# Four attention layers on one core: VectorE's exponentials in the final layer's first chunk taken spaced and in halves, with memory of their own from the second layer on

## The chip, the core and the metric

The kernel runs on one core of a Trainium2 chip. Its engines are TensorE (PE, with its weight loads listed apart as PEld), VectorE (DVE), ScalarE (ACT), GpSimd (POOL) and SyncE (SP), which work side by side, each on its own list of instructions in order. The metric is the device time of one execution in microseconds. Three runs of the kernel before took 2165.64, 2168.42 and 2171.80 us, median 2168.42.

## The reference

Four attention layers follow each other, each with a layer norm in front and a residual sum behind; x has 2048 positions of 640 values, there are 32 heads of 20. The first and third (A) see a window of 256 earlier positions, the second and fourth (B) see all positions.

```python
def _A_ref(x, wqkv, wo):                       # _B_ref is the same without the mask
    qkv = ((x @ wqkv).reshape(B, S, 3, H, Dh)).transpose(2, 0, 3, 1, 4)
    q, k, v = qkv[0], qkv[1], qkv[2]
    scores = jnp.einsum("bhqd,bhkd->bhqk", q, k) * (Dh ** -0.5)
    mask = (idx[:, None] - idx[None, :] >= 0) & (idx[:, None] - idx[None, :] < 256)
    p = _softmax(jnp.where(mask[None, None], scores, -1e9), axis=-1)
    o = jnp.einsum("bhqk,bhkd->bhqd", p, v)
    return o.transpose(0, 2, 1, 3).reshape(B, S, D) @ wo

x = x + _A_ref(_layernorm(x), A_wqkv, A_wo)
x = x + _B_ref(_layernorm(x), B_wqkv, B_wo)
x = x + _A_ref(_layernorm(x), A_wqkv, A_wo)
x = x + _B_ref(_layernorm(x), B_wqkv, B_wo)
```

## The kernel before

Layers are numbered 0 to 3 in the code; 1 and 3 see all keys. Positions are cut into four chunks c of 512, keys into 16 blocks of 128, heads into eight groups g of four. A unit is one (layer, chunk, group), for some units with only a part of the keys: layer 1's chunk 0 is done in four parts of four key blocks, layer 3's chunk 0 in two parts, key blocks 0 to 11 and 12 to 15, since the last chunk of the layer below is finished late. What such a part yields is kept in the tile `raw_o` (L864 to L875) until the last part adds to it.

All units stand in one list (L752 to L768), and a main loop (from L1371) goes through their score banks. A bank is 128 keys by 512 positions for one head. One step of the loop issues the scores of up to three banks on TensorE (L1416), one exponential over all of them on ScalarE (L1442), and, some steps later, the matmuls with the values (L1475). PSUM has eight banks: steps take banks 0 to 2 and 3 to 5 in turn, bank 7 collects the output, and bank 6 is, from the later parts of layer 1's chunk 0 on, the only one for all other work on TensorE.

That other work is a list of tasks, run by `pump`, `choose` and `advance` a little in each step, ordered by when they are needed: layer norm and its transposes (`t_ln`), projections of q, k (`t_block`, matmuls of `by_columns` at L315) and v (`t_v`), and the output projection (`t_out`, sum at L587). Each ends with an eviction from PSUM by VectorE (L339), and the next one can take bank 6 only after it. `rate` sets how much of it a step gets. Where TensorE would have too little to do, `unread` adds matmuls that nobody reads.

VectorE also computes exponentials itself, for a few pairs of banks that are taken from the end of a unit's list (`side_take`), so that ScalarE's step covers two banks instead of three. For one pair VectorE does two conversions to fixed point, one per bank (L989), and a chain of four operations over both banks, 1024 columns: `fraction` (L1005), `square` (L1013), `cubic` (L1017) and `whole` (L1023). The result is used as any other exponential (L1065). Memory of a chain: two tiles `xi` for the fixed-point numbers, one tile `t`, and a list of output tiles. `side_giver` says which unit gives the next pair, `side_work` decides by `state["lag"]`, an estimate of how far VectorE is behind, whether a chain's next operation is issued now.

Before the change there are two regimes. In layer 1 from its chunk 1 on (`side_early`), the chain's memory is all in `raw_o`, which layer 3's first unit needs again; `cubic` and `whole` are issued as two halves of 512 columns, at least GAP_1 = 5 steps lie between two banks taken, and the limits LAG_1, WORK_1 and PRE_1 are low. From layer 3's chunk 0, group 4, on (`side_start`), the memory is in three of the five tiles `xnT` for normalised chunks and in tiles that the windowed layers no longer need; operations are whole, there is no gap, and the limits LAG, WORK are higher. Between them, in layer 3's groups 0 to 3 and in the small units of layer 2 that stand there, VectorE takes no banks.

Of the kernel before, what the change touches and what calls it, by code (L numbers as in the profile page):

```python
# [18 lines left out]
P = 128  # L19
# [5 lines left out]
KD = D // P  # L25
# [20 lines left out]
KEEP = 30  # L46
HALF = True
HALF_3 = False
MOST_1 = 64
# [10 lines left out]
def kernel(  # L60
# [22 lines left out]
    xtp = pool("xtp", 5)  # L83
# [31 lines left out]
    kas = [ka_all[:, n, :] for n in range(KA)]  # L115
    qa_all = big.tile([P, QA, C], BF16, name="qa", tag="qa")
# [211 lines left out]

    def used(l, c):
        users[l, c] -= 1  # L330
        if users[l, c] == 0:
            live["xnT"] -= 1

# [76 lines left out]
    def t_ln(l, c):  # L410
# [19 lines left out]
        xt = xtp.tile([P, KD, C], BF16, name="xnT", tag="xnT")  # L430
# [432 lines left out]
    def finish_unit(u):  # L863
        l, c, g = u.l, u.c, u.g  # L864
        state["lag"] += 0.7
        if u.part and u.part[1] < NT:
            if not part_o:
# [12 lines left out]
        while len(tails) >= 3:  # L880
            require(tails[0].name)
        end = (l, c) == (3, NC - 1) and g >= G - 2
        before = g - 2 if end else g - 3
        if packed(l, c) and before >= 0:
            require(("tail", l, c, before))
        oT = ons[l, c][:, 5 + g % 3 if packed(l, c) and not end else g, :]
        if u.part:
            nc.vector.tensor_tensor(out=oT, in0=part_o["t"][:, g, :], in1=op, op=ALU.add)
        else:
            nc.vector.tensor_copy(out=oT, in_=op)  # L890
        ended_units.append((l, c, g, oT))
# [8 lines left out]
        "xi": deque(), "chain": deque(), "out": deque(), "late": False, "early": False,  # L900
        "half": None, "at": 0, "last": 0,
    }
    givers = [u for u in units if not u.windowed and (u.l, u.c) != (1, 0)]

    def side_tiles(xi, t, outs):

        side["xi"].extend(xi)
        side["t"] = t
        side["out"].extend(outs)

    def side_start():

        assert live["xnT"] <= 2 and not side["chain"] and side["half"] is None
        tl = [xtp.tile([P, KD, C], BF16, name="xnT", tag="xnT") for _ in range(3)]
        live["xnT"] += 3
        f = [v[:, 0:4, :].rearrange("p a b -> p (a b)").bitcast(F32) for v in tl]
        side["xi"].clear()
        side["out"].clear()
        outs = [ka_all[:, KA - 6 + 2 * n : KA - 4 + 2 * n, :] for n in range(3)]
        outs += [qa_all[:, 2 * n : 2 * n + 2, :] for n in range(2)]  # L920
        side_tiles(f[0:2], f[2].bitcast(F16)[:, 0 : 2 * C], outs)
        side["late"] = True

    def side_early():

        b = part_o["t"]
        f = [b[:, 2 * n : 2 * n + 2, :].rearrange("p a b -> p (a b)") for n in range(2)]
        outs = [b[:, n, :].bitcast(BF16).rearrange("p (a b) -> p a b", a=2) for n in range(5, G)]
        side_tiles(f, b[:, 4, :].bitcast(F16), outs)
        side["early"] = True  # L930

    def side_giver():

        if not side["late"] and state["tick"] < side["last"] + GAP_1:
# [3 lines left out]
        if not side["xi"]:  # L938
# [3 lines left out]
        for n in range(side["at"], min(side["at"] + 3, len(givers))):  # L942
# [3 lines left out]
            if not side["late" if u.l == 3 else "early"]:  # L946
                return None
            if u.l == 1 and len(u.aside) >= MOST_1:
                continue
            if len(u.rest) >= (KEEP if len(u.rest) + len(u.aside) < u.size else 12):  # L950
# [46 lines left out]
    def chain(u, xi):  # L997
# [23 lines left out]
        def whole(h):  # L1021
# [5 lines left out]
            if h.stop == 2 * C:  # L1027
                side["xi"].append(xi)
# [3 lines left out]
        halves = (slice(0, C), slice(C, 2 * C)) if HALF and (u.l == 1 or HALF_3) else every  # L1032
# [24 lines left out]
    def side_values(u, wait):  # L1057

        pairs = side_out.get(id(u), ())
        while u.valued < len(pairs) and pairs[u.valued][1] + wait <= state["tick"]:  # L1060
# [8 lines left out]
            side["out"].append(pt)  # L1069
# [166 lines left out]
    def first_ln():  # L1236
# [3 lines left out]
        xt = xtp.tile([P, KD, C], BF16, name="xnT", tag="xnT")  # L1240
# [55 lines left out]
    with tc.manual_schedule():  # L1296
# [74 lines left out]
        while ended is None or t < ended + 8:  # L1371
# [3 lines left out]
            if flow:  # L1375
                if not side["early"] and state["unit"] >= index[1, 1, 0, None]:
                    side_early()
                if (
                    not side["late"] and state["unit"] >= index[3, 0, 4, PARTS[3][0]]
                    and live["xnT"] <= 1 and not live["qa"] and not live["ka"]  # L1380
# [4 lines left out]
                giver = side_giver() if state["lag"] < (LAG if side["late"] else LAG_1) else None  # L1385
# [106 lines left out]
            if n_b and not side["late"]:  # L1492
# [82 lines left out]
```

## Time and profile before

| | |
|---|---|
| median of three runs | 2168.42 us |
| the profiled execution's time | 2167.19 us |
| its span, first to last instruction | 2165.5 us |
| TensorE clock granted, mean share | 0.998 |
| first layer and layer 1's chunk 0 | 0 to 492 us |
| layer 1 from chunk 1, with layer 2's units among it | 492 to 1268 us |
| layer 3, chunk 0, groups 0 to 3, keys 0 to 11 | 1268 to 1354 us |
| layer 2, chunk 3 (eight small units) | 1354 to 1397 us |
| layer 3, chunk 0, groups 4 to 7, keys 0 to 11 | 1397 to 1475 us |
| layer 3, chunk 0, the last four key blocks | 1475 to 1541 us |
| layer 3, chunks 1 to 3 | 1541 to 2155 us |

The stages are found by the exponentials: the steps of the loop, in order, are the exponentials on ScalarE in order of time. A row of the profile's windows has the window, its length, and the busy time of TensorE, of its weight loads, of VectorE, ScalarE and GpSimd. Busy time below the length of the window is time in which that engine stood. A row of waits has the waiting engine and line, who ended the wait, and how long it was in total, how often and at most.

### The profile page before, as it was taken

What the parts mean: (1) busy time and instruction counts of PE and PEld (TensorE: products, weight loads), DVE (VectorE), ACT (ScalarE), POOL (GpSimd) and SP (SyncE); (2) the same over time, 40 slices, a digit from 0 to 9 for tenths busy, and PEclk for the clock granted to TensorE, in tenths of its full rate; (3) what the DMA queues carried; (4) which work ended last, traced back from release to release, by engine and by line L of the source; (5) the groups of instructions that cost most, each with busy time, mean ns of one, the idle gap of its engine ahead of it and who ended that gap; (6) DMA issues with size and microseconds to landing.
All of it is one profiled execution on the core that took longest, in us unless ns stands there. A gap on an engine that the chain in (4) does not pass through costs nothing. (4 is left out here: it accounts for less than half of the span.)

```text
span 2165.5 us, 73279 instructions
## 1 busy us (share of the span) xinstructions
PE 1924.8 (89%) x31759; PEld 754.6 (35%) x31759; DVE 1488.7 (69%) x2625; ACT 2086.1 (96%) x1717; POOL 485.9 (22%) x953
## 2 busy tenths in 40 slices
PE   8999999988889898888988989888898898888898
PEld 4444443433333333333333433332332222222222
DVE  5656665426666776776767733676779887888896
ACT  7889899999999999999999999989999999999997
POOL 6665546110122113410053112511000000000000
PEclk9999999999999999999999999999999999999999
DMA  6223233322211323112241133112121111111100
GB/s 204 76 84 107 75 92 101 81 80 64 79 45 27 84 61 90 41 41 61 56 112 33 37 86 99 39 42 77 53 60 44 35 36 42 32 33 39 42 30 17
DMA packets 88418, 137.29 MB, mean 63 GB/s; under 512 B 20766, under 2 KB 63486, under 8 KB 88094
## 3 DMA queue, kind: packets, MB, share of 16 engines
q1 hardware_dynamic: 68878, 79.43, 13.9%
q0 software_dynamic: 19216, 53.17, 8.3%
q8 instruction: 249, 4.08, 0.8%
q14 instruction: 75, 0.61, 0.1%
HBM read 99.52 MB, written 27.79 MB: 59 GB/s over the span
## 5 line engine op out<-in xcount | busy, mean ns | idle before, releaser
L1442 ACT ACTIVATE pt<-ps 128x1536 bf16<-128x1536 f32 (+2 forms) x1641 | 2051.7, 1406 | 46.4 <-PE ps L1416 35.5
L1416 PE MATMUL ps<-qt,kt 32*128 32x512 bf16 x3914 | 544.6, 383 | 59.8 <-ACT pt L1442 52.5
L315 PE MATMUL ps<-masks,ident 128*32 128x512 bf16 x5652 | 505.6, 384 | 96.6 <-ACT pt L1442 47.5
L1475 PE MATMUL ps<-pt,vt 128*21 128x512 bf16 x3774 | 375.9, 386 | 1.8 <-issue 1.0
L1416 PEld LDWEIGHTS <-kt 32*128 32x128 bf16 x3914 | 154.7, 91 | 460.2 <-issue 440.4
L315 PEld LDWEIGHTS <-ident 128*32 128x32 bf16 x5652 | 180.3, 94 | 278.9 <-issue 253.5
L1515 POOL TENSOR_SCALAR_AFFINE_SELECT pt<-pt 128x256 bf16<-128x256 bf16 (+2 forms) x506 | 217.1, 451 | 187.6 <-ACT pt L1442 175.3
L315 PE MATMUL ps<-xnT,wqk 128*32 128x512 bf16 x3320 | 225.2, 381 | 11.9 <-DMA wqk<-in_B_wqkv_dram 2.1
L339 DVE CAST st<-ps 128x512 bf16<-128x512 f32 x134 | 92.5, 690 | 143.9 <-PE ps L315 143.6
L1475 PEld LDWEIGHTS <-vt 128*21 128x21 bf16 x3774 | 93.4, 89 | 260.1 <-issue 256.3
L989 DVE TENSOR_SCALAR xnT<-ps 128x512 int32<-128x512 f32 x210 | 144.1, 687 | 34.6 <-PE ps L971 27.5
L315 PE MATMUL ps<-wop,on 128*32 128x320 bf16 x3712 | 160.5, 300 | 5.7 <-DVE x_sb L587 3.9
L1526 DVE TENSOR_TENSOR pt<-pt,masks 128x256 bf16<-128x256 bf16 (+3 forms) x268 | 113.4, 438 | 46.5 <-ACT pt L1442 44.3
L315 PEld LDWEIGHTS <-on 128*32 128x32 bf16 x5760 | 122.3, 95 | 63.7 <-issue 29.8
L1416 PE MATMUL ps<-qa,ka 32*128 32x384 bf16 (+2 forms) x1408 | 118.0, 276 | 22.5 <-ACT pt L1442 19.1
L587 DVE TENSOR_TENSOR x_sb<-x_sb,ps 128x320 bf16<-128x320 bf16 x120 | 58.2, 485 | 101.6 <-PE ps L315 101.1
L1185 DVE TENSOR_TENSOR on<-on,ps 128x512 bf16<-128x512 bf16 x128 | 86.4, 684 | 59.2 <-PE ps L315 57.0
L315 PE MATMUL ps<-wv,xnT 128*32 128x320 bf16 x2560 | 116.0, 301 | 9.0 <-DVE vs L339 2.0
L315 PEld LDWEIGHTS <-wqk 128*32 128x32 bf16 x3320 | 83.2, 96 | 96.0 <-issue 38.1
L989 DVE TENSOR_SCALAR raw_o<-ps 128x512 int32<-128x512 f32 x112 | 76.8, 686 | 47.3 <-PE ps L1416 46.8
L890 DVE CAST on<-ps 128x512 bf16<-128x512 f32 x112 | 76.7, 685 | 37.9 <-PE ps L1475 30.7
L554 POOL DMA_DIRECT2D k_d<-st x75 | 42.5, 567 | 225.7 <-DVE st L339 213.0
(99 smaller groups left out, 1797.9 us busy)
## 6 DMA issues: line engine op xcount, KB each, us to landing
vt<-v_d SPq DMA_DIRECT2D x48, 336.0 KB
kt<-k_d SPq DMA_DIRECT2D x192, 80.0 KB
wqk<-in_B_wqkv_dram POOLq DMA_DIRECT2D x80, 160.0 KB, 3.5
wqk<-in_A_wqkv_dram POOLq DMA_DIRECT2D x70, 160.0 KB, 3.6
k_d<-st POOLq DMA_DIRECT2D x75, 128.0 KB, 2.5
q_d<-st POOLq DMA_DIRECT2D x75, 128.0 KB, 2.3
qt<-q_d SPq DMA_DIRECT2D x384, 20.0 KB
v_d<-vs POOLq DMA_DIRECT2D x16, 336.0 KB, 3.0
```

The source lines that it names most:

```text
L315: nc.tensor.matmul(out_[r], lhsT=lhsT[:, r], rhs=rhs, start=start, stop=stop)
L339: nc.vector.tensor_copy(out=out_, in_=in_)
L554: nc.gpsimd.dma_start(out=dst, in_=staging.pop())
L587: nc.vector.tensor_tensor(out=xv, in0=had, in1=yp, op=ALU.add)
L890: nc.vector.tensor_copy(out=oT, in_=op)
L989: nc.vector.tensor_scalar(out=xi.bitcast(I32)[:, i * C : (i + 1) * C], in0=z, scalar1=SCALE * LOG2E * FIX, scalar2=127.5 * FIX, op0=ALU.mu ...
L1185: nc.vector.tensor_tensor(out=oT, in0=oT, in1=zb, op=ALU.mult)
L1416: nc.tensor.matmul(sp[:, i, col * P : (col + qn) * P], lhsT=u.k(kc, j), rhs=u.q(j, q0, qn), start=True, stop=True,)
L1442: nc.scalar.activation(out=pt[:, i:k, b0 * P :], in_=sp[:, i:k, b0 * P :], func=ACT.Exp, scale=SCALE,)
L1475: nc.tensor.matmul(op[32 * j : 32 * j + VW, q0 * P : (q0 + qn) * P], lhsT=u.v(kc, j), rhs=pg[:, i, col * P : (col + qn) * P], start=(first ...
L1515: nc.gpsimd.affine_select(out=v, in_=v, compare_op=ALU.is_gt if later else ALU.is_ge, fill=0.0, base=0, pattern=[[0, k - i], [-1 if later ...
L1526: nc.vector.tensor_tensor(out=pt_[:, i:k, cols], in0=pt_[:, i:k, cols], in1=mv_, op=ALU.mult)
```

## The change

VectorE's exponentials get memory that doesn't depend on `raw_o` being free. The five tiles `xnT` become one tile `xt_all` with five slices that the kernel hands out itself (`take_xt`, `used`). Near the end of layer 1's chunk 0 `side_first` takes three of the slices for good: two `xi`, one `t` and two outputs. When chunk 0 of layer 1 is done, `side_lend` adds the eight slices of `raw_o` as outputs; at layer 3's first unit `side_retire` takes them back, those in use as soon as they come home (`side_home`). `side_start` only adds outputs in the tiles of the windowed layers.

The regime is now chosen by `freely()`, true from layer 3's chunk 1 on. Until then everything is as in layer 1: gap, low limits, halves. So layer 3's groups 0 to 3 and layer 2's last units among them get VectorE exponentials too, and groups 4 to 7 get them spaced and halved. Units of fewer than 32 banks (the last four key blocks) give none. A unit gives its first pair only while it has at least KEEP_1 = 39 banks left (KEEP = 30 from chunk 1 of layer 3 on, as before); the bound MOST_1 is gone. When a unit has fewer than 12 banks left, its chain's limit rises to WORK.

```diff
--- before.py
+++ after.py
@@ -44,9 +44,10 @@
 PRE = 1.3
 PRE_1 = 0.8
 KEEP = 30
+KEEP_1 = 39
 HALF = True
+BEFORE = 0
 HALF_3 = False
-MOST_1 = 64
 GAP_1 = 5
 QA = 4
 
...
@@ -113,6 +113,7 @@
     qts = [big.tile([P, C], BF16, name=f"qt{n}", tag=f"qt{n}") for n in range(4)]
     ka_all = big.tile([P, KA, C], BF16, name="ka", tag="ka")
     kas = [ka_all[:, n, :] for n in range(KA)]
+    xt_all = big.tile([P, 5, KD, C], BF16, name="xnT", tag="xnT")
     qa_all = big.tile([P, QA, C], BF16, name="qa", tag="qa")
     qas = [qa_all[:, n, :] for n in range(QA)]
 
@@ -326,10 +327,19 @@
 
     users = {}
 
+    xt_free = deque(range(5))
+    xt_n = {}
+
+    def take_xt(l, c):
+
+        xt_n[l, c] = xt_free.popleft()
+        return xt_all[:, xt_n[l, c]]
+
     def used(l, c):
         users[l, c] -= 1
         if users[l, c] == 0:
             live["xnT"] -= 1
+            xt_free.append(xt_n.pop((l, c)))
 
     def evac(out_, in_):
         if state["act"]:
...
@@ -886,6 +897,8 @@
         oT = ons[l, c][:, 5 + g % 3 if packed(l, c) and not end else g, :]
         if u.part:
             nc.vector.tensor_tensor(out=oT, in0=part_o["t"][:, g, :], in1=op, op=ALU.add)
+            if l == 1 and g == G - 1:
+                side_lend()
         else:
             nc.vector.tensor_copy(out=oT, in_=op)
         ended_units.append((l, c, g, oT))
@@ -897,45 +910,67 @@
 
     side_out = {}
     side = {
-        "xi": deque(), "chain": deque(), "out": deque(), "late": False, "early": False,
-        "half": None, "at": 0, "last": 0,
+        "xi": deque(), "chain": deque(), "out": deque(), "late": False, "on": False,
+        "half": None, "at": 0, "last": 0, "lent": None,
     }
-    givers = [u for u in units if not u.windowed and (u.l, u.c) != (1, 0)]
-
-    def side_tiles(xi, t, outs):
-
-        side["xi"].extend(xi)
-        side["t"] = t
+    givers = [u for u in units if not u.windowed]
+    away = []
+
+    def side_home(kind, v):
+
+        if any(v is a for a in away):
+            away[:] = [a for a in away if a is not v]
+        else:
+            side[kind].append(v)
+
+    def side_retire(parts):
+
+        for v in parts:
+            for kind in ("xi", "out"):
+                if any(v is a for a in side[kind]):
+                    side[kind] = deque(a for a in side[kind] if a is not v)
+                    break
+            else:
+                away.append(v)
+
+    def side_first():
+
+        for n in range(2, 5):
+            xt_free.remove(n)
+        live["xnT"] += 3
+        f = xt_all[:, 2:5].rearrange("p n a b -> p (n a b)")
+        f = [f[:, n * 2 * C : (n + 1) * 2 * C] for n in range(7)]
+        b = xt_all[:, 2:5].rearrange("p n a b -> p (n a b)")
+        outs = [f[n].rearrange("p (a b) -> p a b", a=2) for n in (5, 6)]
+        side["xi"].extend(b[:, 4 * n * C : 4 * (n + 1) * C].bitcast(F32) for n in range(2))
+        side["t"] = f[4].bitcast(F16)
         side["out"].extend(outs)
+        side["on"] = True
+
+    def side_lend():
+
+        b = part_o["t"]
+        side["lent"] = [b[:, n, :].bitcast(BF16).rearrange("p (a b) -> p a b", a=2) for n in range(G)]
+        side["out"].extend(side["lent"])
 
     def side_start():
 
-        assert live["xnT"] <= 2 and not side["chain"] and side["half"] is None
-        tl = [xtp.tile([P, KD, C], BF16, name="xnT", tag="xnT") for _ in range(3)]
-        live["xnT"] += 3
-        f = [v[:, 0:4, :].rearrange("p a b -> p (a b)").bitcast(F32) for v in tl]
-        side["xi"].clear()
-        side["out"].clear()
         outs = [ka_all[:, KA - 6 + 2 * n : KA - 4 + 2 * n, :] for n in range(3)]
         outs += [qa_all[:, 2 * n : 2 * n + 2, :] for n in range(2)]
-        side_tiles(f[0:2], f[2].bitcast(F16)[:, 0 : 2 * C], outs)
+        side["out"].extend(outs)
         side["late"] = True
 
-    def side_early():
-
-        b = part_o["t"]
-        f = [b[:, 2 * n : 2 * n + 2, :].rearrange("p a b -> p (a b)") for n in range(2)]
-        outs = [b[:, n, :].bitcast(BF16).rearrange("p (a b) -> p a b", a=2) for n in range(5, G)]
-        side_tiles(f, b[:, 4, :].bitcast(F16), outs)
-        side["early"] = True
+    def freely():
+
+        return state["unit"] >= index[3, 1, 0, None]
 
     def side_giver():
 
-        if not side["late"] and state["tick"] < side["last"] + GAP_1:
+        if not freely() and state["tick"] < side["last"] + GAP_1:
             return None
         if side["half"] is not None:
             return side["half"][0]
-        if not side["xi"]:
+        if not side["xi"] or not side["on"]:
             return None
         while side["at"] < len(givers) and not givers[side["at"]].rest:
             side["at"] += 1
@@ -943,11 +978,9 @@
             u = givers[n]
             if id(u) not in loaded or state["tick"] < loaded[id(u)] + 8:
                 return None
-            if not side["late" if u.l == 3 else "early"]:
-                return None
-            if u.l == 1 and len(u.aside) >= MOST_1:
+            if u.size < 32:
                 continue
-            if len(u.rest) >= (KEEP if len(u.rest) + len(u.aside) < u.size else 12):
+            if len(u.rest) >= ((KEEP if freely() else KEEP_1) if len(u.rest) + len(u.aside) < u.size else 12):
                 side["at"] = n
                 return u
         return None
@@ -1025,22 +1058,24 @@
                 in1=q[:, h], op0=ALU.mult, op1=ALU.add,
             )
             if h.stop == 2 * C:
-                side["xi"].append(xi)
+                side_home("xi", xi)
                 side_out.setdefault(id(u), []).append((box["out"], state["tick"]))
 
         every = (slice(0, 2 * C),)
-        halves = (slice(0, C), slice(C, 2 * C)) if HALF and (u.l == 1 or HALF_3) else every
+        halves = (slice(0, C), slice(C, 2 * C)) if HALF and not freely() else every
         cost = 0.7 if len(halves) == 2 else 1.25
         steps = [(fraction, h, 0.7) for h in every] + [(square, h, 0.7) for h in every]
         steps += [(cubic, h, cost) for h in halves] + [(whole, h, cost) for h in halves]
-        return deque(steps)
+        return deque(s + (u,) for s in steps)
 
     def side_work(force, limit=None):
 
         if limit is None:
-            limit = WORK if side["late"] else WORK_1
+            limit = WORK if freely() else WORK_1
         while side["chain"]:
-            step, h, cost = side["chain"][0][0]
+            step, h, cost, u = side["chain"][0][0]
+            if len(u.rest) < 12:
+                limit = max(limit, WORK)
             if step.__name__ == "square" and not side["out"]:
                 return False
             if not force and state["lag"] + cost > limit:
@@ -1066,7 +1101,7 @@
                     op[32 * j : 32 * j + VW, :], lhsT=u.v(kc, j), rhs=pt[:, i, :], start=False,
                     stop=True, skip_group_check=True,
                 )
-            side["out"].append(pt)
+            side_home("out", pt)
             u.valued += 1
 
     def side_push():
...
@@ -1373,16 +1408,22 @@
             state["tick"] += 1
             n_b = 0
             if flow:
-                if not side["early"] and state["unit"] >= index[1, 1, 0, None]:
-                    side_early()
+                if (
+                    not side["on"] and state["unit"] >= index[1, 0, G - 1, PARTS[1][3]]
+                    and all(n in xt_free for n in range(2, 5)) and live["xnT"] <= 2
+                ):
+                    side_first()
+                if side["lent"] and state["unit"] >= index[3, 0, 0, PARTS[3][0]] - BEFORE:
+                    side_retire(side["lent"])
+                    side["lent"] = None
                 if (
                     not side["late"] and state["unit"] >= index[3, 0, 4, PARTS[3][0]]
-                    and live["xnT"] <= 1 and not live["qa"] and not live["ka"]
+                    and not live["qa"] and not live["ka"]
                 ):
                     side_start()
                 if state["unit"] >= final:
                     last_tick[0] = 0
-                giver = side_giver() if state["lag"] < (LAG if side["late"] else LAG_1) else None
+                giver = side_giver() if state["lag"] < (LAG if freely() else LAG_1) else None
                 if giver is not None and state["unit"] >= final and (
                     state["held"] is not None or mfree[6][0] > state["tick"]
                     or state["want"] >= state["tick"] - 1
@@ -1489,7 +1530,7 @@
                     closed = t
                     break
 
-            if n_b and not side["late"]:
+            if n_b and not freely():
                 side_work(False, PRE_1)
             if n_b and not state["early"]:
                 background(t, n_b)
```

More of the change, by code (lines that the diff above doesn't have):

```diff
@@ L82 @@
     vap = pool("vap", 10)
-    xtp = pool("xtp", 5)
     onp = pool("onp", 2)
@@ L429, in t_ln @@
         )
-        xt = xtp.tile([P, KD, C], BF16, name="xnT", tag="xnT")
+        xt = take_xt(l, c)
         def normed(i):
@@ L866, in finish_unit @@
         if u.part and u.part[1] < NT:
+            assert l == 1 or side["late"] or not away
             if not part_o:
@@ L1239, in first_ln @@
         live["xnT"] += 1
-        xt = xtp.tile([P, KD, C], BF16, name="xnT", tag="xnT")
+        xt = take_xt(0, 0)
         def warm(count):
```

## The prediction

> **What bounds the kernel now.** I read the engine shares first, then the stages, the waits of the worst stage, the order of time within it, and the prices of VectorE's operations.
>
> ```profile
> span 2165.5 us, 73279 instructions
> PE 1924.8 (89%) x31759; PEld 754.6 (35%) x31759; DVE 1488.7 (69%) x2625; ACT 2086.1 (96%) x1717; POOL 485.9 (22%) x953
> ```
>
> ACT is the bound: it is busy 2086.1 of 2165.5 us. Whatever leaves its work as it is can win only from the 79 us in which it stands. Of these 47 lie before 492 us and 10 after the last exponential, which the change doesn't touch. The stages show where the rest lies (columns: window, its length, busy time of PE, weight loads, VectorE, ACT and GpSimd):
>
> ```profile
> core 0: us, PE busy (x) PEld busy (x) DVE busy (x) ACT busy (x) POOL busy (x), PEclk, DMA share, GB/s
> ...
> 743.00:853.00 110.00, 99.74 (x1532) 39.13 (x1532) 73.11 (x133) 109.53 (x87) 23.20 (x36) 1.00 0.32 85
> 1203.00:1268.00 65.00, 57.94 (x978) 24.10 (x978) 42.64 (x83) 62.21 (x49) 11.69 (x18) 1.00 0.25 68
> ...
> 1268.00:1354.00 86.00, 77.42 (x1246) 31.40 (x1242) 27.91 (x58) 85.98 (x65) 18.57 (x30) 1.00 0.33 88
> 1354.00:1397.00 43.00, 35.68 (x753) 15.81 (x746) 24.38 (x56) 43.00 (x34) 28.88 (x63) 1.00 0.15 41
> 1397.00:1475.00 78.00, 67.80 (x1146) 28.41 (x1146) 59.78 (x100) 70.11 (x57) 12.57 (x20) 1.00 0.20 55
> 1475.00:1541.00 66.00, 55.57 (x831) 19.84 (x827) 45.25 (x69) 63.98 (x52) 6.72 (x10) 1.00 0.25 65
> 1541.00:1747.00 206.00, 185.63 (x2513) 58.90 (x2513) 175.51 (x230) 204.50 (x152) 0.00 (x0) 1.00 0.15 42
> ```
>
> The first two rows are the second layer, whose VectorE exponentials are already spaced and halved: ACT stands 0.5 us of 110, and 2.8 of 65. The next four are the final layer's first chunk: A, units 0 to 3 (1268 to 1354); B, the third layer's last small units (to 1397); C, units 4 to 7 (to 1475); D, the part over the last keys (to 1541). In A and B ACT never stands and VectorE is at 0.32 and 0.57; in C and D, where all of this chunk's VectorE exponentials lie, ACT stands 7.9 and 2.0 us. No engine is full in C: a coupling costs there, and the waits name it.
>
> ```profile
> ACT pt L1442 <- PE ps L1416: 8.8, 15, 1.3
> ...
> PE ps L315 <- DVE x_sb L587: 2.8, 4, 1.3
> PE ps L315 <- DVE st L339: 2.7, 4, 1.4
> PE ps L315 <- DVE vs L339: 2.4, 4, 1.2
> ```
>
> ACT waits for scores (8.8 us between 1397 and 1500), and PE, which takes its work in order, had stood before them until VectorE emptied the one bank that the background has. What VectorE did meanwhile, in order of time:
>
> ```profile
> 1443.03 1.21 DVE L1017 SCALAR_TENSOR_TENSOR qa<-qa,xnT 128x1024 f16<-128x1024 f16 x1
> 1444.16 0.48 DVE L339 CAST vs<-ps 128x320 bf16<-128x320 f32 x1
> 1444.56 1.21 DVE L1023 SCALAR_TENSOR_TENSOR qa<-xnT,qa 128x1024 uint16<-128x1024 int32 x1
> 1445.91 0.69 DVE L989 TENSOR_SCALAR xnT<-ps 128x512 int32<-128x512 f32 x1
> 1446.52 0.48 DVE L339 CAST vs<-ps 128x320 bf16<-128x320 f32 x1
> ```
>
> Each 0.48 us eviction stands behind a 1.21 us step of a chain.
>
> **The change part by part.** Both kernels' main loops take 1612 steps, nearly always one exponential on ACT each (counted, like all that is said here of the changed kernel, in the order of its instructions). A pair is two 512-column banks that VectorE turns into exponentials and ACT doesn't. By stage, pairs go from 56, 0, 0, 8, 6, 91 (second and third layer up to A; A; B; C; D; the last three chunks) to 57, 6, 3, 4, 0, 92: in all 161 to 162. So ACT's work hardly changes. Price of a step of three banks: 86.0 us over A's 64 steps, 1.344; a pair is two thirds of that, 0.9. Price of a pair on VectorE:
>
> ```profile
> L1023 DVE SCALAR_TENSOR_TENSOR ka<-xnT,ka 128x1024 uint16<-128x1024 int32 x63 | 76.8, 1220 | 1.1
> ...
> L1017 DVE SCALAR_TENSOR_TENSOR ka<-ka,xnT 128x1024 f16<-128x1024 f16 x63 | 76.8, 1218 | 0.8
> L1023 DVE SCALAR_TENSOR_TENSOR raw_o<-raw_o 128x512 uint16<-128x512 int32 x112 | 75.2, 684 | 0.0
> L1017 DVE SCALAR_TENSOR_TENSOR raw_o<-raw_o 128x512 f16<-128x512 f16 x112 | 74.3, 688 | 1.1
> ```
>
> Whole: 2 x 0.687 (fixed point) + 0.69 + 0.69 + 1.22 + 1.22 = 5.2 us. Halved: 2 x 0.69 + 2 x 0.68 in place of 2.44, so 5.5. Fourteen more pairs are halved (70 against 56): 4.3 us more VectorE work.
>
> Stage A. Six pairs come in: 91648 columns instead of 98304, 59.7 full steps, 80.2 us of ACT. PE loses nothing (a pair's scores and values are still its own) and gets 40 more background matmuls, two projections, at 225.2/3320 = 0.068 us: 77.4 + 2.7 = 80.1. So PE takes ACT's place here. It has nowhere been full: 0.906 over the fullest long stage with pairs (743 to 853), 0.96 at best over 14 us without any:
>
> ```profile
> 1311.00:1325.00 14.00, 13.46 (x286) 6.59 (x278) 5.90 (x12) 13.99 (x11) 0.00 (x0) 1.00 0.21 61
> ```
>
> VectorE goes from 28 to some 64 us: the six pairs with the tail of one begun before are 13 and 14 half steps, 12 of the short whole ones and 12 fixed points, 9 + 9.6 + 8.3 + 8.2 = 35, and two more evictions 1.4. Ends: 80.2 (ACT's own time) and 80.1/0.906 = 88.4. I take a PE share of 0.94, nearer the rows of this very stage: 85.2 against 86.0, -0.8.
>
> Stage B. Three pairs in: 46592 columns, 30.3 steps, 40.8 us; PE is at 0.83 here and partly fills. ACT stands 0.5 to 2% where such small units have pairs today (0.5 us of 92 in 853 to 945, 1.7 of 92 in 1111 to 1203), so 0.5: 41.3 against 43.0 for its 32 steps at A's price, -1.7. Ends -2.2 and 0.
>
> Stage C. Pairs go from 8 to 4: 81920 columns, 71.7 us of ACT, and the standing time on top, 7.9 now. With spaced halves it was 0.5% (743 to 853) to 4.3% (1203 to 1268, the stage whose PE and VectorE shares are nearest); I take 4.5 us, over the upper one because VectorE has, in the new order, as much to do in C as now, about 60 us, against its 0.66 of the time in both those stages: 76.2 against 78.5, -2.3. Ends 72.0 and 79.6 (nothing gained).
>
> Stage D. All six pairs leave: 51 full steps, 68.5 us, against 66.2 now: +2.3. This is the bill for A and B, and nearly certain, as the like steps in A run without a stop.
>
> Outside these: one more pair before A, one more in the last chunks, where ACT stands 1.5 of 206 us: -0.9 each, ends 0 and -0.9. The second layer's pairs shift by a few steps (its counts stay 18, 19, 19 a chunk): 0, ends +2 and -2, since ACT stands there 8.8 us of 776 and an offset can move a part of it.
>
> The rest costs nothing: no DMA is added or removed on SP or GpSimd and ACT, PE and VectorE carry the same number of waits within 1%. The five normalised chunks become slices of one tile, and three are given to the chain from the second layer on; never more than two chunks live at once from there in either kernel, so no layer norm waits; if that cover went, the next chunk's projections would be pressed into fewer steps. The eight slices of raw_o that the chain borrows go back before the final layer's first unit is finished; its first write there would wait for the last values matmul of a pair, which lies a unit (25 us) back. GpSimd gets 5 instructions more for masks, under cover (29 of 43 us in B).
>
> [...] The two rows give 0.15 us per cut. [...]
>
> Sum: -0.8 - 1.7 - 2.3 + 2.3 - 0.9 - 0.9 = -4.3 us. The profiled execution took 2167.2 (span 2165.5 and 1.7 around it), 1.2 under the median 2168.4. Against the median: 2164.1.
>
> **The rivals.**
> First: the coupling goes almost wholly, as in 743 to 853. A at 81.5, B at 40.9, C at 72.0, D +2.3: -4.5 - 2.1 - 6.5 + 2.3 - 1.8 = -12.6, 2156. For it: nine spaced pairs cost 0.5 us there. Against: A then needs PE at 0.98. Half of this surplus gives 2160.
> Second, on the other side: VectorE becomes the brake in A. Its share goes to 64/85 = 0.75, C's is 0.77, and A has a projection in nearly every step. If evictions queue there as in C today (ACT 12.25 of 14 us in 1452 to 1466, 0.875), A takes 80.2/0.875 = 91.7, +5.7, and if C keeps its 7.9, +1.1, with B at 0, D +2.3 and -1.8: +7.3, 2175.7. It decides (over 6.5 us in all) once ACT stands more than 10.7 us in A. For it: load, not spacing, would be the cause. Against: a halved step blocks an eviction 0.69 us, not 1.22.
> Third: the change does not do what it says. The standing time only moves, from C and D to A, 10 us in all as now, or the 4.3 us of the halves lie on the path: 2167 to 2168.
>
> **How the numbers follow.** A measurement can tell about 0.3% (6.5 us) from no change. My forecast, within that, 0.40; the third rival, also within, 0.16; the first or its upper half (2162 and less) 0.28; the second 0.16, of which a part reaches past 2175. The range, 2155 to 2176, goes from the first rival's end to the second's.
>
> **What would show it.** Right: VectorE's 512-column steps over A and B; ACT standing 3 to 6 us in A with PE at 0.93 or more; C standing under 5; D without a stop; ACT's busy time about 1 to 2 us less in all. Wrong: ACT standing 8 us or more in A behind PE that waits for evictions (L339, L587), or standing in the second layer well over 9 us, or a first write of raw_o in the final layer that waits.

## The result, and the profile after

The changed kernel takes 2179.82 us (median of 6 runs, 2177.0 to 2183.1), the kernel before 2167.55 on the same chip: 1.0055 of it, 95% interval 1.0042 to 1.0067. It is slower, by about 12 us; 2164 were forecast, 2176 was the range's end. The page after:

```profile
span 2177.3 us, 73576 instructions
PE 1935.8 (89%) x31878; PEld 759.9 (35%) x31879; DVE 1500.9 (69%) x2664; ACT 2087.2 (96%) x1720; POOL 491.4 (23%) x958
```

ACT's work is the same to 1.1 us. Nearly all of the loss is time in which ACT stands. By stage (the columns as before; the windows begin and end near the same steps of the main loop as in the table of the kernel before):

```profile
491.00:1279.00 788.00, 697.55 (x11678) 283.41 (x11670) 547.61 (x1040) 772.65 (x630) 176.95 (x328) 1.00 0.22 60
1279.00:1368.00 89.00, 80.35 (x1279) 32.74 (x1275) 62.04 (x112) 82.28 (x65) 20.78 (x33) 1.00 0.33 91
1368.00:1409.00 41.00, 34.66 (x723) 15.66 (x720) 29.59 (x60) 41.00 (x34) 28.03 (x57) 1.00 0.13 33
1409.00:1486.00 77.00, 70.04 (x1206) 29.63 (x1206) 54.43 (x106) 73.48 (x58) 14.78 (x25) 1.00 0.21 56
1486.00:1554.00 68.00, 56.58 (x863) 20.74 (x862) 16.68 (x33) 68.00 (x52) 6.73 (x10) 1.00 0.25 67
```

The kernel before, with the second layer's row whole (its other stages stand in the prediction):

```profile
487.00:1268.00 781.00, 693.39 (x11630) 282.16 (x11622) 541.65 (x1031) 772.19 (x627) 175.51 (x325) 1.00 0.23 61
```

Start to start of the same steps of the main loop, in us:

| stage | before | after | difference | forecast |
|---|---|---|---|---|
| first layer, layer 1's chunk 0 | 471.8 | 475.4 | +3.6 | 0 |
| "second layer": layer 1's chunks 1 to 3, with layer 2's units | 780.4 | 787.6 | +7.2 | -0.9, within -2.9 and +2 |
| A: final layer's units 0 to 3 | 86.1 | 89.2 | +3.0 | -0.8 |
| B: third layer's last small units | 43.0 | 40.6 | -2.4 | -1.7 |
| C: units 4 to 7 | 78.4 | 77.0 | -1.4 | -2.3 |
| D: the last four key blocks | 66.0 | 68.2 | +2.2 | +2.3 |
| final layer's chunks 1 to 3, to its last step | 611.0 | 610.6 | -0.4 | -0.9 |

The part that the change is about, A to D, comes out at +1.4. A step is not quite the same work in both kernels: units 0 to 3 begin at step 959 after the change and 958 before, units 4 to 7 at 1057 and 1054. Cut where the units begin, B wins nothing (43.3 against 43.0 us), C is 5.9 us shorter, and A to D in all is 0.2 us shorter, with 8.9 us lost ahead of it. Three fifths of the loss are in the second layer, whose pairs were to shift by a few steps only; 1.4 of its 7.2 us are one stretch of 3.4 us at 1134.5 in which TensorE's clock was granted at half (0.51 from 1134.5 to 1137.9; eight steps with it took 14.02 us, and 12.57 in the run below that has the same order there and no such stretch). ACT's waits there, after and before (waiting engine and line, releaser: total, times, longest):

```profile
ACT pt L1483 <- PE ps L1457: 12.7, 28, 1.3
```

```profile
ACT pt L1442 <- PE ps L1416: 6.6, 17, 1.3
```

The matmul that ACT waits for is late because PE stood in order before it. At 546 us in the changed kernel VectorE, PE and ACT, in order of time:

```profile
545.64 0.68 DVE L1046 TENSOR_TENSOR raw_o<-xnT 128x1024 f16<-128x1024 f16 x1
546.35 1.29 DVE L1050 SCALAR_TENSOR_TENSOR raw_o<-raw_o,xnT 128x512 f16<-128x512 f16 x2
547.56 0.48 DVE L349 COPY xnT<-ps 128x640 bf16<-128x640 bf16 x1
```

```profile
546.71 0.40 PE L1516 MATMUL ps<-pt,vt 128*21 128x512 bf16 x4
548.10 0.46 PE L316 MATMUL ps<-wv,xnT 128*32 128x320 bf16 x8 [1.00 <-DVE xnT L349]
548.49 0.39 PE L1457 MATMUL ps<-qt,kt 32*128 32x512 bf16 x3
```

```profile
548.99 3.71 ACT L1483 ACTIVATE pt<-ps 128x1536 bf16<-128x1536 f32 x3 [0.58 <-PE ps L1457]
```

A square and two halves of a cubic stand together on VectorE; the eviction of a layer norm's transposes waits behind them; the next task's matmul waits 1.00 us for it, the scores stand behind that matmul, and ACT stops for 0.58 us at 548.99. The halves were there, but nothing lay between them. In the kernel before, the same layer norm meets a chain whose operations alternate with the evictions:

```profile
540.61 0.43 DVE L435 TENSOR_SCALAR xn<-x_sb,rstd,nmr 128x640 bf16<-128x640 bf16 x1
541.47 0.49 DVE L339 COPY xnT<-ps 128x640 bf16<-128x640 bf16 x1 [0.43 <-PE ps L455]
541.88 0.68 DVE L1013 TENSOR_TENSOR raw_o<-raw_o 128x1024 f16<-128x1024 f16 x1
542.74 0.49 DVE L339 COPY xnT<-ps 128x640 bf16<-128x640 bf16 x1 [0.18 <-PE ps L455]
543.15 0.68 DVE L1017 SCALAR_TENSOR_TENSOR raw_o<-raw_o 128x512 f16<-128x512 f16 x1
```

### The profile page after: what moved, and what is told of

Its sections match the earlier page's. It is cut to its first block, busy times and chain, and to the rows that moved or that the text cites. A ratio compares the mean times of both kernels' runs of the same rounds, so it can differ in the third digit from the quotient of the medians.

```text
span 2177.3 us, 73576 instructions
## 1 busy us (share of the span) xinstructions
PE 1935.8 (89%) x31878; PEld 759.9 (35%) x31879; DVE 1500.9 (69%) x2664; ACT 2087.2 (96%) x1720; POOL 491.4 (23%) x958
## 5 line engine op out<-in xcount | busy, mean ns | idle before, releaser
L1483 ACT ACTIVATE pt<-ps 128x1536 bf16<-128x1536 f32 (+3 forms) x1644 | 2052.4, 1404 | 54.9 <-PE ps L1457 44.4
L316 PE MATMUL ps<-masks,ident 128*32 128x512 bf16 x5772 | 516.7, 384 | 92.3 <-ACT pt L1483 46.6
L1022 DVE TENSOR_SCALAR xnT<-ps 128x512 int32<-128x512 f32 x324 | 222.5, 687 | 66.3 <-PE ps L1457 38.5
L1556 POOL TENSOR_SCALAR_AFFINE_SELECT pt<-pt 128x256 bf16<-128x256 bf16 (+2 forms) x511 | 222.0, 458 | 200.1 <-ACT pt L1483 188.1
L1567 DVE TENSOR_TENSOR pt<-pt,masks 128x512 bf16<-128x512 bf16 (+4 forms) x273 | 115.3, 439 | 45.2 <-ACT pt L1483 43.1
L1038 DVE TENSOR_SCALAR xnT<-xnT 128x1024 f16<-128x1024 int16 x162 | 114.2, 705 | 3.6
```

The source lines that it names most:

```text
L316: nc.tensor.matmul(out_[r], lhsT=lhsT[:, r], rhs=rhs, start=start, stop=stop)
L1022: nc.vector.tensor_scalar(out=xi.bitcast(I32)[:, i * C : (i + 1) * C], in0=z, scalar1=SCALE * LOG2E * FIX, scalar2=127.5 * FIX, op0=ALU.mu ...
L1038: V.tensor_scalar(out=t[:, h], in0=low[:, h], scalar1=T1, scalar2=T0, op0=ALU.mult, op1=ALU.add)
L1483: nc.scalar.activation(out=pt[:, i:k, b0 * P :], in_=sp[:, i:k, b0 * P :], func=ACT.Exp, scale=SCALE,)
L1556: nc.gpsimd.affine_select(out=v, in_=v, compare_op=ALU.is_gt if later else ALU.is_ge, fill=0.0, base=0, pattern=[[0, k - i], [-1 if later ...
L1567: nc.vector.tensor_tensor(out=pt_[:, i:k, cols], in0=pt_[:, i:k, cols], in1=mv_, op=ALU.mult)
```

## The experiments

The two halves of the change and its memory were taken apart first, then the second layer's new rules, then the place of the pairs alone.

**The second layer as before, the final layer as changed.**

```diff
+MOST_1 = 64
...
-    givers = [u for u in units if not u.windowed]
+    givers = [u for u in units if not u.windowed and (u.l, u.c) != (1, 0)]
...
+            if u.l == 3 and state["unit"] < index[3, 0, 0, PARTS[3][0]]:
+                return None
+            if u.l == 1 and len(u.aside) >= MOST_1:
+                continue
-            if len(u.rest) >= ((KEEP if freely() else KEEP_1) if ...
+            if len(u.rest) >= ((KEEP if freely() or u.l == 1 else KEEP_1) if ...
...
-            if len(u.rest) < 12:
+            if u.l == 3 and len(u.rest) < 12:
...
-                    not side["on"] and state["unit"] >= index[1, 0, G - 1, PARTS[1][3]]
+                    not side["on"] and state["unit"] >= index[1, 1, 0, None]
```

> The second layer's pairs taken at exactly the steps of before (and from the same units), the final layer's first chunk as in the changed kernel, the memory of the changed kernel. Theory S (the 7 us lost between 491 and 1279 us come from the pairs' new places in the second layer): that stretch goes back to about 780 us, and the whole to within 4 us of before, about 2169. Theory M (the loss comes from the one tile with five slices, whatever the order): the stretch stays near 787 and the whole near 2179. Theory F (the loss is made in the final layer's first chunk, units 0 to 3, and what the second layer shows is chance): the whole stays 5 us or more over before, with units 0 to 3 at 89 us.

The edit also lends the chain one slice of raw_o instead of eight, so that the second layer has three output tiles as before; the run of the memory alone has this too. Measured: 1.0006 (0.9995 to 1.0017). Second layer 780.4 us, A to D 88.8, 40.6, 76.7, 68.2: +0.8 us in all there. Theory S holds; F falls, since the loss in A is nearly paid back in B and C.

**The second layer as changed, the final layer as before.**

```diff
     def freely():
-        return state["unit"] >= index[3, 1, 0, None]
+        return side["late"]
...
-            if u.size < 32:
+            if u.l == 1 and u.size < 32:
                 continue
+            if u.l == 3 and not side["late"]:
+                return None
...
-            if len(u.rest) < 12:
+            if u.l == 1 and len(u.rest) < 12:
...
-        halves = (...) if HALF and not freely() else every
+        halves = (...) if HALF and u.l == 1 else every
```

> The other half alone: the second layer's pairs as in the changed kernel, the final layer's first chunk as before (pairs from group 4 on, whole operations, no gap). Theory S: the second layer's stretch near 787 us, the final layer's first chunk 273.5 us in all as before, the whole about 7 to 10 us over before. Theory M: the same time as the changed kernel or nearly, 2177 to 2180. Theory F: within 4 us of before.

Measured: 1.0047 (1.0029 to 1.0064); second layer 788.9 us, A to D 86.1, 43.1, 78.1, 66.0. The second layer alone brings nearly the whole loss, and the two halves add up: 0.47 + 0.06 against 0.55%.

**The memory alone.** Both edits above together: every instruction at its step of before, only the tiles are the changed kernel's.

> Every instruction at the step of before; only the memory is the changed kernel's: one tile with five slices for the normalised chunks, the chain in three of them from the second layer on. Theory M: 2175 us or more. Theories S and F: within 0.15% of before. The first 487 us, whose instructions are the same in all kernels of this study, tell what chance alone does: half clock stretches there in some runs and not in others would show that the 3.6 us which the changed kernel's profiled run lost there are not its own.

Measured: 1.0001 (0.9991 to 1.0010); 780.2 in the second layer. The tiles cost nothing, theory M falls. So it is the order. What lending eight slices instead of one does to the order was not tried alone.

**Whole operations in the final layer's first chunk.**

```diff
-        halves = (...) if HALF and not freely() else every
+        halves = (...) if HALF and u.l == 1 else every
```

> The changed kernel with the final layer's first chunk spaced but not halved: cubic and whole over 1024 columns there. If it is the load on VectorE and PE that makes units 0 to 3 stand (89.2 us against 86.1), the 4 us of VectorE work that fall away give 1 to 3 us back. If it is the time for which one operation blocks an eviction (1.22 against 0.69 us), units 0 to 3 get longer by 2 us or more, and the whole is at 2181 or over.

Measured: 1.0059 (1.0037 to 1.0082), not to be told from the changed kernel as a whole. By stage, against the changed kernel: A 87.6 for 89.2, B 40.8 for 40.6, C 80.3 for 77.0, with two half clock stretches of 3.4 us in C (0.50 granted in each). The expectation of the load came true in A, that of the blocked evictions did not. But the edit moves a pair too: A has five pairs here and C five, where the changed kernel has six and four. So what halving alone costs in A or wins in C is not shown.

**The second layer's new rules, one at a time.** From the changed kernel: no raised limit at a unit's end; the old bound of 30 banks (it holds for a unit that has begun; one that has not may give down to 12 in all kernels); the start where before had it.

```diff
-            if len(u.rest) < 12:
+            if u.l == 3 and len(u.rest) < 12:
```

> The changed kernel without its rule that raises the chain's limit when a unit has fewer than 12 banks left, in the second layer only. Theory R (this rule lets several operations of a chain follow each other, and evictions wait behind them): the second layer's stretch falls from 787 us to 782 or less. Theory P (where the pairs stand against layer norms and projections decides, whatever moved them; the places of before are a good draw): it lands anywhere between 781 and 790, with its stops at other steps. Theory K (the bound of 39 banks): stays at 786 or more.

```diff
-            if len(u.rest) >= ((KEEP if freely() else KEEP_1) if ...
+            if len(u.rest) >= ((KEEP if freely() or u.l == 1 else KEEP_1) if ...
```

> The changed kernel with the old bound of 30 banks (in place of 39) for a unit of the second layer that has begun. Theory K: the stretch falls to 782 or less. Theory R: stays at 786 or more, since the rule is still there. Theory P: anywhere between 781 and 790, with stops at other steps than in the changed kernel.

```diff
-    givers = [u for u in units if not u.windowed]
+    givers = [u for u in units if not u.windowed and (u.l, u.c) != (1, 0)]
...
-                    not side["on"] and state["unit"] >= index[1, 0, G - 1, PARTS[1][3]]
+                    not side["on"] and state["unit"] >= index[1, 1, 0, None]
```

> The changed kernel, but the second layer's first pair allowed only where before allowed it, so that the first pairs stand one to two steps later than in the changed kernel (steps 356, 366, 377 instead of 355, 365, 375). From about step 703 of the main loop on the order is the changed kernel's again. Theories R and K: no part of the loss comes back, 786 us or more. Theory P: the part up to step 703 changes by 1 us or more in either direction, and the part behind it, which has the same order, stays the same to 0.1 us apart from half clock stretches.

Measured, whole and second layer: without the raised limit 1.0030 (1.0017 to 1.0042), 784.2 us; with 30 banks 1.0036 (1.0022 to 1.0050), 791.1; with the old start 1.0038 (1.0023 to 1.0053), 785.9. Theory K falls. By these times theory R misses its 782, too, but in the second layer the first of these runs has two half clock stretches of 3.4 us, the second run three such lengths, the third none. Cut into pieces of twenty steps from step 346, the run without the raised limit loses 3.9 us to before in the three pieces that such a stretch touches, and nothing (-0.1) in all the others; the changed kernel loses 5.1 us outside its one such piece.

The place shown above says the same. Steps 386 to 406 took 25.05 us before, 26.57 changed, 25.19 without the raised limit, 25.91 with the old start (27.48 with 30 banks holds a half clock stretch). In the run without the raised limit the pair is taken at the same step as in the changed kernel, but no half of the cubic stands between the square and the eviction of the transposes:

```profile
540.20 0.68 DVE L1046 TENSOR_TENSOR raw_o<-xnT 128x1024 f16<-128x1024 f16 x1
541.06 0.49 DVE L349 COPY xnT<-ps 128x640 bf16<-128x640 bf16 x1 [0.18 <-PE ps L465]
541.47 0.68 DVE L1050 SCALAR_TENSOR_TENSOR raw_o<-raw_o,xnT 128x512 f16<-128x512 f16 x1
```

So the raised limit, which puts operations of a chain together, is not excluded as a main cause of the changed kernel's loss in the second layer: at this place it is the cause. How much of the whole it holds, one profile with two half clock stretches does not tell. The same run's A, with six halved pairs in another order, took 91.8 us without such a stretch, against 89.2.

Of the run with the old start, the part up to step 703 took 452.2 us, 0.7 less than the changed kernel, where 1 or more either way was expected. The part that was to stay the same (from step 703) took 333.7 us, where the run with the changed second layer alone had 335.0; most stretches of eight steps agree to 0.01 us, four differ by 0.4 to 0.8. These misses were not followed further.

**The kernel before, moved.** Nothing of the change is in these three; the second layer's first pair comes one, three and six steps later (the bound is 351, 353 and 356).

```diff
-                if not side["early"] and state["unit"] >= index[1, 1, 0, None]:
+                if not side["early"] and state["unit"] >= index[1, 1, 0, None] and t >= 353:
```

> The kernel before with the second layer's first pair one step later (step 357 instead of 356). Theory P (any other places cost, before's are a good draw): the second layer's stretch 2 us or more over the 780.3 of before, with the added stops at steps where pairs have moved. Against it: within 1 us of 780.3.

> The kernel before with one thing changed: the second layer's first pair may come only three steps later (at step 359 instead of 356), so that the pairs behind it move by about three steps each; same regime, rules, memory. Theory P: the second layer's stretch gets 3 us or more longer than the 780.3 of before (785 to 790), without any rule of the change. Theories R and K: it stays within 2 us of 780.3, as none of the new rules is in it.

> The kernel before with the second layer's first pair six steps later (362 instead of 356); from step 676 of the main loop on all pairs stand again where before has them, and there are as many. Theory P: up to step 676 (448.7 us for steps 346 to 703 in before) 1 us or more longer, and behind it the same to 0.1 us apart from half clock stretches. Against it: no change in either part, within 0.3 us.

Measured: 1.0028 (1.0016 to 1.0040), 1.0030 (1.0013 to 1.0047) and 1.0032 (1.0019 to 1.0045); second layer 786.0, 785.1 and 784.6 us. With six steps, all of it lies where the pairs are moved: 418.3 against 414.2 us up to step 676, and 366.3 as in before from there. The rows of one and six steps:

```profile
491.00:1277.00 786.00, 695.48 (x11648) 283.34 (x11641) 546.68 (x1040) 772.18 (x628) 175.30 (x325) 1.00 0.22 60
```

```profile
492.00:1276.00 784.00, 696.72 (x11630) 282.29 (x11630) 540.38 (x1033) 771.58 (x629) 176.96 (x326) 1.00 0.22 61
```

The same ACT work as before (772 us), 12 to 14 us of standing instead of 9. The moves of one and three steps have one pair more in the second layer (57), the move of six has 56 as before. In all seven orders tried other than that of before, the second layer takes 784 to 791 us, in part with half clock stretches, which the four profiles with the order of before don't have there:

| order | second layer | over before | in pieces of twenty steps with a half clock stretch | in all others |
|---|---|---|---|---|
| changed | 787.6 | +7.2 | 2.1 | 5.1 |
| without the raised limit | 784.2 | +3.8 | 3.9 | -0.1 |
| 30 banks | 791.1 | +10.7 | 5.9 | 4.8 |
| old start | 785.9 | +5.5 | 0 | 5.5 |
| before, one step later | 786.0 | +5.6 | 2.2 | 3.4 |
| before, three steps later | 785.1 | +4.7 | 2.3 | 2.4 |
| before, six steps later | 784.6 | +4.2 | 0 | 4.2 |

Theory P holds for the kernel before: the places of before are a good draw (or were searched for; the runs cannot tell), and three moves without any rule of the change cost 2.4 to 4.2 us outside those pieces.

**The chain without its halves' work.** All instructions at the changed kernel's steps, but up to the final layer's second chunk two of the chain's four operations are left out.

```diff
         def cubic(h):
             q = box["q"]
+            if len(halves) == 2:
+                return
...
-            V.scalar_tensor_tensor(
-                out=q.bitcast(U16)[:, h], in0=xi.bitcast(I32)[:, h], scalar=1.0 / C,
+            if len(halves) == 1:
+                V.scalar_tensor_tensor(...)
```

> The changed kernel with every instruction at its step, but the two halved operations (cubic and whole, both halves) are not computed up to the final layer's second chunk, so those exponentials are left as the square: 2.7 of a pair's 5.5 us of VectorE work fall away. Theory V (PE and then ACT stop because evictions stand behind the chain's operations): the second layer's stretch falls from 787 us by 4 or more, to 783 or less, and the final layer's units 0 to 3 from 89.2 to 87 or less. Theory T (the stops come from PE's own load at those steps, with one bank for all background work): the stretch stays at 786 or more, units 0 to 3 at 89.

Measured: 1.0002 (0.9988 to 1.0016), the time of before; second layer 778.6 us, A 89.8. The windows of this run (second layer, A) and its two waits of the second layer to hold against those after:

```profile
488.00:1267.00 779.00, 695.59 (x11678) 284.93 (x11671) 410.75 (x814) 771.20 (x630) 174.26 (x328) 1.00 0.23 61
1267.00:1357.00 90.00, 81.66 (x1281) 33.62 (x1278) 46.78 (x85) 82.75 (x66) 20.66 (x33) 0.98 0.33 89
```

```profile
ACT pt L1486 <- PE ps L1460: 5.4, 16, 0.8
...
PE ps L316 <- DVE xnT L349: 2.1, 8, 0.4
```

```profile
PE ps L316 <- DVE xnT L349: 5.4, 11, 1.0
```

The second fence is this run's, the third the changed kernel's. In the second layer theory V holds: with the same order on every engine, VectorE's operations taken away give back 9.0 us (1.4 of them the half clock stretch, which this run doesn't have there), ACT's waits for scores fall from 12.7 to 5.4, PE's for the transposes' evictions from 5.4 to 2.1. In A the expectation of theory T came true: VectorE's work falls from 62.0 to 46.8 us and the stage stays at 89.8 (a half clock stretch of 3.4 us lies in it, 0.51 granted). So it is not the cubic and the whole that make A long. That PE's own load does is argued, not shown: PE is busy 0.90 of A, and the same six pairs in another order took 91.8 us above with 80.5 us of PE work.

**A version from the balance.** Second layer as before, no pairs in A, spaced halves in B and C, and D gives pairs again (to the first edit above, `index[2, NC - 1, 0, None]` as the bound and the size rule for layer 1 alone).

> A version made from the stages' balance: the second layer's pairs exactly as before; in the final layer's first chunk no pairs in units 0 to 3 (where they cost 3 us), spaced and halved ones from the third layer's last small units on (where they won 2.4), and the last four key blocks give pairs again. Pairs by stage 56, 0, 3, 5, 3, 92, two fewer in all than before. If the stages add up: third layer's last units -2.4 us, units 4 to 7 -1 to -2, the last key blocks 0 to +1.5, the rest -0.4: 2164 to 2166 where before has 2168, a gain of 0.1 to 0.2%.

Measured: 0.9997 (0.9987 to 1.0008). A to D 86.1, 40.4, 78.0, 67.7 against 86.1, 43.0, 78.4, 66.0: the 2.5 us of B are there, but D gave back 1.7 and C won 0.3, with a half clock stretch inside it (0.98 granted from 1394 to 1472.5). The 2164 to 2166 were not reached (2167.4 against 2167.7 of before); no version here beats the kernel before.

## Why the prediction was wrong

The step that failed is the sentence "The second layer's pairs shift by a few steps (its counts stay 18, 19, 19 a chunk): 0, ends +2 and -2". It took the few stops of a layer that is at 0.99 of ACT as nearly independent of place: an offset was to move a part of 8.8 us of standing, 2 us at most. The memory run and the two half runs show that the second layer's order alone brings nearly the whole loss (0.47 of 0.55%), and the three moved kernels that the count of pairs says little and the place much: with the same 56 pairs, six steps cost 4.2 us. The run without cubic and whole shows how: with the same order, 9.0 us come back when these operations don't stand before the evictions. And the second layer's pairs were not only shifted: the raised limit, the bound of 39 banks, the earlier start and the longer list of outputs act there too, and the prediction priced none of them; the raised limit is what put the operations together at 546 us. A wider end could have come from the worst stretch of a like stage: the 2.8 us of 65 that 1203 to 1268 shows, carried over the 780 us of the layer, gives some 34 us of standing at the most (an estimate), where the layer had 8.8. With such an end the loss would have lain within the range. To take the placement as nearly free of cost because the regime is the same was the error, and no rival named it; only one of the signs of being wrong (standing well over 9 us) pointed at it.

Point by point:

- ACT's work: 2087.2 against 2086.1 us; 1 to 2 us less were forecast and 1.1 more came, which is small beside the loss.
- A: that PE takes ACT's place was the author's estimate; the runs do not show it. PE's busy time came out at 80.35 us where the sum had 80.1. But the share was mis-sized: 0.94 was chosen, 80.35/89 = 0.90 came, the row of the fullest long stage, so 89.2 us against 85.2. The upper end, 88.4, was nearer. ACT stood 6.7 us there, where 3 to 6 were to show the forecast right and 8 to show it wrong. The second rival put this on VectorE (load 62 us, 64 forecast); the run without cubic and whole shows that it is not the load of these two operations. Why PE is not busy for a tenth of A was not settled.
- B, C, D: -2.4, -1.4, +2.2 against -1.7, -2.3, +2.3. Right in sign and near in size, by equal steps; the sum took 66.2 us for D before, where the table has 66.0. C stands 3.5 us after, under the 4.5 taken, but has 70.0 us of PE work to do where it had 67.8.
- The halves: two operations of 512 columns took VectorE 2 x 0.69 us where one of 1024 took 1.22, 0.15 us more, by the rows of the kernel before. With whole operations A was 1.6 us faster and C 3.3 us slower, but one pair had moved from A to C and two half clock stretches lie in that C. The sum took nothing as lost by the halves, and as a whole the two kernels cannot be told apart.
- Memory, waits, DMAs cost nothing: right for the tiles, 1.0001, with one slice of raw_o lent instead of eight.
- What would show it wrong: "standing in the second layer well over 9 us" came true, 15.4 us against 8.8.
- The first 490 us: +3.6 in this pair of profiles, with the same instructions. Over the fourteen profiled executions of this study that stretch took 470.2 to 479.2 us: 470.2 to 472.9 with two lengths of half clock in it, 474.9 to 479.2 with three to eight. The changed kernel's profile had three, that of before two. It is chance, and no part of the change.

Of the 11.8 us between the two profiles: 7.2 the second layer's order, with the half clock stretch in it, 1.4 A to D, 3.6 chance in the first stretch, -0.4 behind. The half runs put the first at 0.47% (0.29 to 0.64, so 6 to 14 us; four executions) and the second at 0.06%; the 7.2 lie within that. How the second layer's loss divides between the raised limit and the other places stays open.

## What to carry to other kernels

Here in-order engines share one buffer for background work, and the time of a stage hung on which operation stands next to which: an edit that only moved work by a few steps was not free (six steps in the kernel before: 4.2 us). Cost such an edit from the worst like stage, not from the mean, and list which of the new rules act in the stages that you take as unchanged. Move the schedule of the untouched kernel by a step or two before crediting or blaming a change; here three such moves cost 0.3% each. Look for half clock stretches before you compare two profiles' stages; here two of them lie in the stage of the run that was to tell what one rule costs. And a stage that is full on one engine need not gain from its relief: A's busy time on ACT fell from 86.0 to 82.3 us, and the stage got 3 us longer.

## What the runs showed of the hardware

Equal orders mostly repeat to about 0.01 us over twenty steps: steps 366 to 386 took 25.01 us in the kernel before and in the memory run, and 25.17 in three runs with the changed second layer (the miss from step 703 on, above, is the exception). What was seen to differ between runs of one order is the TensorE clock: in single stretches of 3.4 us, or two or three of them in a row, it is granted at half. Most lie in the first 500 us, and there they come at like places: near 90 us in all fourteen profiles (from 89.4 in the kernel before, from 96.9 in the changed one) and near 217 us in twelve (from 219.8 in the changed one). The changed kernel's windows of 3.4 us around the one at 1134.5:

```profile
1127.70:1131.10 3.40, 2.94 (x82) 1.44 (x74) 2.01 (x7) 2.94 (x3) 1.98 (x5) 1.00 0.47 124
1131.10:1134.50 3.40, 1.76 (x32) 0.81 (x30) 3.08 (x7) 3.06 (x3) 2.64 (x5) 1.00 0.19 57
1134.50:1137.90 3.40, 3.40 (x44) 1.13 (x41) 0.75 (x2) 1.60 (x2) 2.87 (x7) 0.51 0.56 150
```

PE was busy for 1.76 of 3.4 us, and the next window ran at 0.51. In each of the fourteen traces the clock changes on a grid of 3.413 us; the changed kernel's half clock stretches begin at 52.52, 96.89, 219.77 and 1134.55 us, 13, 36 and 268 such lengths apart. On that grid, from 20 to 2140 us, 53 times a window at full clock was followed by one at half, and PE had been busy for 0.94 to 2.38 us in the window ahead. Every window at full clock with less than 1.88 us of PE work was followed so (28 windows); from 1.88 to 2.38 us it was 25 of 180; with more it was none. So in these traces a window in which PE was busy for under 1.88 of 3.413 us was charged twice, by its own length and by the half clock after it. What the half clock cost can be read where an equal order ran with and without it: 1.45 and 0.72 us in steps 846 to 866 (the changed kernel and the run with whole operations against the run with the changed second layer alone), 0.93 and 0.91 us in steps 526 to 546. That the half clock follows from the activity in the window ahead is read from the traces and was not tried by an experiment.
